# Two more chunks transposed by DMA instead of TensorE in a retention layer with a feed-forward block

## The chip, the cores and the metric

The kernel runs on one core of a Trainium2 chip. The metric is the time of one execution on the device in microseconds (us); where several executions were timed, their median is given. Engines are called as the profile calls them: PE is TensorE (PEld its weight loads), DVE is VectorE, ACT is ScalarE, POOL is GpSimd, and SP is the engine whose queue issues nearly all DMAs.

## The reference: what is computed

A recurrent retention layer (4 batches, 8 heads, 768 steps, head dimension 64) feeds a two-layer block with the activation h - tanh(h).

```python
gamma = 1.0 - 2.0 ** (-5.0 - np.arange(H))            # one decay for each head
for t in range(S):
    state = gamma * state + outer(k[:, :, t], v[:, :, t])
    y[:, :, t] = scale * (q[:, :, t] @ state)
x = y.transpose(0, 2, 1, 3).reshape(B * S, H * D)      # 3072 tokens of 512
h = x @ w_in                                           # 512 x 2048
out = (h - np.tanh(h)) @ w_out                         # 2048 x 512
```

q, k and v are float32. The two weight matrices arrive as 64-bit floats; the kernel converts them to float32 itself, in 32 tiles, with ACT, DVE and POOL.

## The kernel before

The 3072 tokens are 24 chunks of 128. For each chunk the kernel loads k, q and v, scales q and v by powers of the decay, and then needs k and q with the head dimension on the partitions (`kqT`), because the score products contract over it. There are two ways to get `kqT`.

With TensorE, as the kernel before does for chunks 0 to 7: eight transposes into a PSUM tile, and a copy out of it by ACT.

```python
    def turn(ci, which, early=False):          # which: 0 for k, 1 for q
        ...
            if which == 0:
                turned[ci] = banks("t", f"kqTp_{ci}")      # PSUM, tag "t" has one buffer
            tp = turned[ci][:, which]
        ...
        for p in range(NP):                    # NP = 4
            nc.tensor.transpose(tp[:, ts(p, P)],
                                t[:, ds(2 * p, 2)].rearrange("p h d -> p (h d)"), ident)

    def turn_copy(ci, which=None):
        ...
            nc.scalar.copy(out=t, in_=turned[ci].rearrange("p i (n t) -> p i n t", n=NP))
```

By DMA, as it does for chunks 8 to 23: ACT separates the 16-bit halves of the float32 words into `apart`, of which there is one buffer; one DMA stores them to a scratch in HBM; a second, transposing DMA reads the scratch and writes `kqT`.

```python
    def turn_by_dma(ci):
        apart = mid.tile([P, 2, 2, H * D], U16, tag="apart", name=f"apart_{ci}", bufs=1)
        for which in range(2):
            words = loaded[ci][which].rearrange("p h d -> p (h d)").bitcast(U16)
            nc.scalar.copy(out=apart[:, :, which],
                           in_=words.rearrange("p (n two) -> p two n", two=2))
        rows = dram.tile([P, 2, 2 * H * D], U16, tag="rows", name=f"rows_{ci}")
        nc.sync.dma_start(out=rows, in_=apart.rearrange("p two i n -> p two (i n)"))
        sides[ci] = mid.tile([P, 2, NP, P], F32, tag="kqT", name=f"kqT_{ci}")   # two buffers
        nc.sync.dma_start_transpose(
            out=sides[ci].rearrange("p i n t -> p (i n) t").bitcast(U16),
            in_=rows.rearrange("p two n -> (p two) n"),
        )
```

The chunk's further way: `products` (the k-v products, which do not read `kqT`, and then the scores, which do), `mask` and `state` on DVE, `outputs` and `outputs_rest` on TensorE, and `keep_x`, an ACT copy of the finished chunk into `xT`, from which the first layer's matmuls (`up`) read.

```python
    def products(ci):
        ...
                    nc.tensor.matmul(halves[...], kh[r, h], vh[r, h], ...)                       # L298
        ...
                    nc.tensor.matmul(halves[...], kT[r, p, ts(a, D)], qT[r, p, ts(a, D)], ...)   # L304

    def keep_x(ci):
        ...
        nc.scalar.copy(out=xT[n][:, :, ts(nj, P)]..., in_=y_banks[:, ci % 2]...)                 # L393

    def up(n, m2, i):
        ...
        keep_busy(hp[:, :P])
        for c in range(NC):
            nc.tensor.matmul(hp, w1[:, c, ts(2 * m2 + i, P)], xT[n // 2][:, c, ts(n % 2, TH)], ...)
```

`keep_busy` issues matmuls on a constant tile into a PSUM place that is about to be overwritten; their number is set by an `x` piece ahead of it. Chunks 4 to 7 are the tokens of `xT[1]`, and steps 4 and 5 of the feed-forward block read chunks 4 and 5.

Every engine runs its instructions in the order in which the program gives them. For the first eight chunks and the first steps of the feed-forward block that order is a string. A letter is a function, the number a chunk, weight tile or step: L loads a chunk, W a weight tile; s and w scale q and v; t and T transpose k and q on TensorE; c and C copy them out; p products, m mask, z state, b outputs, e a small read of the output by ACT, r the rest of the outputs, y keep_x; A, D, G convert a weight tile on ACT, DVE, POOL; u and v the two halves of `up`; a and q the activations of a step on ACT, d and g its DVE part; o the second layer's matmuls; E their sum; x idle matmuls.

```python
    order = """
    ...
    C4 r3 g0 L5 y3 x1 p4 A4 W5 u2 D3 s5 v2 W6 w5 m4 D4 u1 G3 a2 q2 z4 L6 x6 t5 d2 G4 T5 A5
    v1 W7 C5 g2 b4 s6 a1 W8 p5 w6 e4 u3 D5 q1 v3 m5 A6 G5 z5 r4 L7 a3 t6 d1 b5 W9 y4 T6 e5
    o0 s7 g1 C6 w7 A7 W10 D6 q3 r5 t7 W11 T7 D7 G6 y5 C7 x3 u4 d3 v4 G7 A8 g3 p6 a4 o1 A9 m6
    z6 q4 D8 p7 E1 d4 G8 b6 o2 e6 m7 g4 A10 r6 z7 u5 y6 D9 b7 v5 D10 G9 e7 r7 a5 o3 y7 q5
    G10 u6 E3 d5 A11 v6 g5 o4 a6 D11 q6 u7 G11 d6 v7 g6 o5 a7 q7 E5 d7 g7 W12 L8 W13 W14
    """
```

After this string a loop runs the other 88 steps and calls `turn_by_dma` for chunks 8 to 23.

Of the kernel before, what the change touches and what calls it, by code (L numbers as in the profile page):

```python
# [32 lines left out]
def kernel(  # L33
# [223 lines left out]
    def turn_copy(ci, which=None):  # L257
        if ci not in sides:
            sides[ci] = mid.tile([P, 2, NP, P], F32, tag="kqT", name=f"kqT_{ci}")
        t = sides[ci]  # L260
        if which is None:
            nc.scalar.copy(out=t, in_=turned[ci].rearrange("p i (n t) -> p i n t", n=NP))
        else:
            nc.scalar.copy(out=t[:, which],
                           in_=turned[ci][which].rearrange("p (n t) -> p n t", n=NP))
# [277 lines left out]
    def tall(ci):  # L543
# [8 lines left out]
        "T": lambda c: turn(c, 1, c < EARLY_TURNS),  # L552
        "c": lambda c: turn_copy(c, 0),
        "C": lambda c: turn_copy(c, 1 if c < EARLY_TURNS else None),
        "p": products,
        "m": mask,
        "z": state,
# [21 lines left out]
    m1 z1 y0 A1 D0 L2 x4 b1 t2 e1 c2 G0 r1 s2 y1 D1 x3 T2 w2 L3 u0 C2 W2 p2 G1 s3 t3 m2 T3  # L579
    w3 c3 v0 z2 C3 b2 A2 L4 p3 e2 W3 D2 a0 r2 s4 y2 w4 q0 W4 m3 z3 G2 x9 t4 b3 A3 d0 T4 e3  # L580
    C4 r3 g0 L5 y3 x1 p4 A4 W5 u2 D3 s5 v2 W6 w5 m4 D4 u1 G3 a2 q2 z4 L6 x6 t5 d2 G4 T5 A5
    v1 W7 C5 g2 b4 s6 a1 W8 p5 w6 e4 u3 D5 q1 v3 m5 A6 G5 z5 r4 L7 a3 t6 d1 b5 W9 y4 T6 e5
    o0 s7 g1 C6 w7 A7 W10 D6 q3 r5 t7 W11 T7 D7 G6 y5 C7 x3 u4 d3 v4 G7 A8 g3 p6 a4 o1 A9 m6
    z6 q4 D8 p7 E1 d4 G8 b6 o2 e6 m7 g4 A10 r6 z7 u5 y6 D9 b7 v5 D10 G9 e7 r7 a5 o3 y7 q5
    G10 u6 E3 d5 A11 v6 g5 o4 a6 D11 q6 u7 G11 d6 v7 g6 o5 a7 q7 E5 d7 g7 W12 L8 W13 W14
    """
# [101 lines left out]
```

## Time and profile before

| | before |
|---|---|
| time, median of 3 | 752.62 us (752.61 to 753.97) |
| span of the profiled execution | 752.1 us |
| PE busy | 740.9 us (99%) |
| DVE busy | 518.0 us (69%) |
| ACT busy | 389.4 us (52%) |
| POOL busy | 126.9 us (17%) |
| mean granted clock of TensorE | 0.998 |

The profile lists for each engine the busy time, and for groups of instructions the line of the kernel, the tile written and the tile read. A timeline gives start and length of merged instructions, and in brackets the idle time before them with what ended it. A table of stretches gives, for each, the busy time and number of instructions of an engine, the clock that TensorE was granted (1.00 is full), the busy share of the DMA engines and the rate. Engines that are idle without being the bottleneck cost nothing by that.

### The profile page before, as it was taken

Reading aid. Unit: us, or ns where it says so; the run is one execution under the profiler, and the core shown is the slowest. Engines: PE = TensorE matmul, PEld = TensorE weight load, DVE = VectorE, ACT = ScalarE, POOL = GpSimd, SP = SyncE. Lnnn points to the kernel's source line nnn. Section 1 sums busy time; section 2 is a strip of 40 time slices with the busy share of each in tenths; the row PEclk is TensorE's granted clock in tenths of the full one; section 3 lists DMA queues with packets and bytes.
Section 4 is the critical chain, followed back from the end, with each engine's and each line's share of the span. In section 5 each row is a group of like instructions: output and inputs, shape, how many; then the busy total and the mean of one; then the engine's idle time right before and its main releaser. Section 6 shows DMA issues by size and latency. Waiting matters only on the chain.

```text
span 752.1 us, 13885 instructions
## 1 busy us (share of the span) xinstructions
PE 740.9 (99%) x5502; PEld 509.9 (68%) x5502; DVE 518.0 (69%) x807; ACT 389.4 (52%) x727; POOL 126.9 (17%) x108
## 2 busy tenths in 40 slices
PE   8899999999999999999999999999999999999997
PEld 7786667666767676766676676666666666666775
DVE  4889989998898666656565656565665666656653
ACT  4567576667665546445545545444344434434442
POOL 0565445445444111100111100000000000000000
PEclk9999999999999999999999999999999999999999
DMA  9972436556553353343342421000000000000000
GB/s 196 234 182 74 127 89 172 158 158 153 156 128 84 99 155 107 67 96 93 91 99 71 98 58 56 29 1 1 29 0 1 28 1 0 29 0 1 28 2 28
DMA packets 125680, 59.76 MB, mean 79 GB/s; under 512 B 109872, under 2 KB 118576, under 8 KB 125616
## 3 DMA queue, kind: packets, MB, share of 16 engines
q1 hardware_dynamic: 125328, 58.67, 29.9%
q8 instruction: 43, 0.70, 0.4%
q10 hardware_dynamic: 288, 0.21, 0.1%
q14 instruction: 21, 0.17, 0.1%
HBM read 35.80 MB, written 14.68 MB: 67 GB/s over the span
## 4 chain that ended last, share of the span: by engine, by line
PE 96%; DMA 2%; DVE 1%; SPq 1%; ACT 0%; issue 0%; ACTq 0%; DVEq 0%
PE h L414 44%; PE o L462 42%; PE y L352 3%; PE o L470 2%; PE s L298 2%; PE s L304 1%; PE kqTp L212 1%; PE kqTp L250 1%; DMA raw<-in_moe_w_in_dram 1%; DMA k<-in_k_dram 1%; SPq L229 1%; DMA out_dram<-sum 0%; SPq L154 0%; DVE power L187 0%; DVE head L185 0%; DVE a L311 0%
## 5 line engine op out<-in xcount | busy, mean ns | idle before, releaser
L414 PE MATMUL h<-xT,w 128*128 128x256 f32 x1536 | 349.9, 381 | 0.0
L414 PEld LDWEIGHTS h<-xT,w 128*128 128x128 f32 x1536 | 289.7, 190 | 68.4 <-issue 31.8
L462 PE MATMUL o<-w,g 128*128 128x512 f32 x736 | 331.9, 593 | 0.0
L462 PEld LDWEIGHTS o<-w,g 128*128 128x128 f32 x736 | 139.4, 190 | 135.1 <-issue 128.4
L423 ACT ACTIVATE u<-h 128x512 f32<-128x512 f32 x96 | 57.3, 597 | 289.0 <-PE h L414 288.9
L439 DVE TENSOR_TENSOR th<-h,th 128x512 f32<-128x512 f32 x96 | 66.3, 690 | 176.0 <-ACT th L424 176.0
L453 DVE COPY_PREDICATED g<-large,th 128x512 f32<-128x512 int32 x96 | 71.8, 748 | 10.2 <-DVE g L452 0.5
L442 DVE SCALAR_TENSOR_TENSOR h<-q,h 128x512 f32<-128x512 f32 x96 | 66.8, 696 | 10.4 <-DVE h L440 0.5
L448 DVE SCALAR_TENSOR_TENSOR h<-q,h 128x512 f32<-128x512 f32 x96 | 66.6, 694 | 8.2
L431 ACT ACTIVATE q<-u,tab 128x512 f32<-128x512 f32 x96 | 69.4, 722 | 0.0
L432 ACT ACTIVATE q<-u,tab 128x512 f32<-128x512 f32 x96 | 69.1, 720 | 0.0
L433 ACT ACTIVATE large<-u,tab 128x512 f32<-128x512 f32 x96 | 68.8, 717 | 0.0
L452 DVE TENSOR_TENSOR g<-h,u 128x512 f32<-128x512 f32 x96 | 66.3, 691 | 3.3
L440 DVE SCALAR_TENSOR_TENSOR h<-u,h 128x512 f32<-128x512 f32 x96 | 65.8, 685 | 0.0
L236 POOL TENSOR_TENSOR q<-q,tab 128x512 f32<-128x512 f32 x22 | 24.3, 1104 | 198.4 <-DMA q<-in_q_dram 115.1
L424 ACT ACTIVATE th<-h 128x512 f32<-128x512 f32 x96 | 56.9, 592 | 0.0
L195 POOL TENSOR_TENSOR low<-low,power 128x512 f32<-128x512 f32 x30 | 38.5, 1282 | 103.1 <-DVE power L187 89.1
L199 POOL TENSOR_TENSOR w<-low,head 128x512 f32<-128x512 f32 x30 | 38.7, 1289 | 2.4
L352 PEld LDWEIGHTS y<-a,v 64*64 64x64 f32 x768 | 15.8, 134 | 16.7 <-ACT large L433 10.6
L236 POOL TENSOR_TENSOR v<-v,tab 128x512 f32<-128x512 f32 x22 | 26.5, 1207 | 0.1
L382 ACT COPY seen<-y 64x1 f32<-64x1 f32 x96 | 10.1, 153 | 28.2 <-PE y L352 27.8
L393 ACT COPY xT<-y 128x512 f32<-128x512 f32 x24 | 14.1, 587 | 17.0 <-PE y L352 17.0
(54 smaller groups left out, 412.8 us busy)
## 6 DMA issues: line engine op xcount, KB each, us to landing
rows<-apart SPq DMA_DIRECT2D x16, 512.0 KB, 2.8
k<-in_k_dram SPq DMA_DIRECT2D x24, 256.0 KB, 4.3
q<-in_q_dram SPq DMA_DIRECT2D x24, 256.0 KB, 4.9
v<-in_v_dram SPq DMA_DIRECT2D x24, 256.0 KB, 5.1
raw<-in_moe_w_out_dram SPq DMA_DIRECT2D x12, 512.0 KB, 3.6
out_dram<-sum SPq DMA_DIRECT2D x23, 256.0 KB, 2.1
raw<-in_moe_w_in_dram SPq DMA_DIRECT2D x14, 256.0 KB, 4.2
raw<-in_moe_w_in_dram SPq DMA_DIRECT2D x28, 128.0 KB, 3.9
```

The source lines that it names most:

```text
L414: nc.tensor.matmul(hp, w1[:, c, ts(2 * m2 + i, P)], xT[n // 2][:, c, ts(n % 2, TH)], start=(i == 0 and c == 0), stop=(c == NC - 1), skip_g ...
L423: nc.scalar.activation(u, hp, AF.Square)
L431: nc.scalar.activation(q0, u, AF.Square, bias=bias0)
L432: nc.scalar.activation(q1, u, AF.Square, bias=bias1, scale=math.sqrt(A))
L433: nc.scalar.activation(large, u, AF.Relu, bias=bias_m)
L439: nc.vector.tensor_tensor(th, hp, th, op=ALU.subtract)
L440: nc.vector.scalar_tensor_tensor(hp, in0=u, scalar=R, in1=hp, op0=ALU.subtract, op1=ALU.mult, reverse0=True)
L442: nc.vector.scalar_tensor_tensor(hp, in0=q0, scalar=C0, in1=hp, op0=ALU.add, op1=ALU.mult)
L448: nc.vector.scalar_tensor_tensor(hp, in0=q1, scalar=A * C1, in1=hp, op0=ALU.add, op1=ALU.mult)
L452: nc.vector.tensor_tensor(flat, hp, u, op=ALU.mult)
L453: nc.vector.copy_predicated(flat, large.bitcast(I32), th)
L462: nc.tensor.matmul(o_p[j], gT[n, m2][:, i, ts(j, P)], w2[:, 2 * m2 + i], start=(first and i == 0), stop=(last and i == 1))
```

## The change

Chunks 6 and 7 are transposed by DMA too: the pieces t6, T6, C6 and t7, T7, C7 go, and K6 and K7, which call `turn_by_dma`, come in. The load of chunk 7 and the loads of weight tiles 9, 10 and 11 are moved ahead of K6, so that on the SP queue they are issued before the store of chunk 6 to the scratch and the transposing DMA behind it. The aim is to take 16 transposes off TensorE, which is busy nearly all the time, and to spare ACT two copies out of PSUM.

```diff
         "C": lambda c: turn_copy(c, 1 if c < EARLY_TURNS else None),
+        "K": turn_by_dma,
         "p": products,
...
-    v1 W7 C5 g2 b4 s6 a1 W8 p5 w6 e4 u3 D5 q1 v3 m5 A6 G5 z5 r4 L7 a3 t6 d1 b5 W9 y4 T6 e5
-    o0 s7 g1 C6 w7 A7 W10 D6 q3 r5 t7 W11 T7 D7 G6 y5 C7 x3 u4 d3 v4 G7 A8 g3 p6 a4 o1 A9 m6
+    v1 W7 C5 g2 b4 s6 a1 W8 p5 w6 e4 u3 D5 q1 L7 W9 W10 W11 K6 v3 m5 A6 G5 z5 r4 a3 d1 b5 y4 e5
+    o0 s7 g1 w7 A7 D6 q3 K7 r5 D7 G6 y5 x3 u4 d3 v4 G7 A8 g3 p6 a4 o1 A9 m6
```

## The prediction

> **What bounds the kernel now.** I read the page first, then who waits for whom on TensorE (PE), then the chain of work in order of time around the places that the change touches, and last the timelines of ACT and of the SP queue there. The busy line of the page:
>
> ```profile
> PE 740.9 (99%) x5502; PEld 509.9 (68%) x5502; DVE 518.0 (69%) x807; ACT 389.4 (52%) x727; POOL 126.9 (17%) x108
> ```
>
> The span is 752.1 us, so PE stands still for only 11. The waits of PE say where: these are the longest two.
>
> ```profile
> PE kqTp L212 <- DVE state L327: 2.9, 1, 2.9
> PE y L352 <- issue: 1.5, 1, 1.5
> ```
>
> Both fall before 32 us. In the window from 40 us to the end, PE waits 0.5 us in all. So PE is the bound wherever the change works: what it takes off PE is gained in full, and what makes PE wait is lost in full, with no later slack to win it back. The chain in order of time (start, length, what) around the removed transposes:
>
> ```profile
> 54.66 0.39 PE y L352 x16
> 55.05 0.59 PE kqTp L250 x4
> 55.64 0.86 PE y L352 x48
> 56.50 0.59 PE kqTp L250 x4
> 57.09 3.44 PE o L462 x8
> 60.52 0.39 PE y L352 x16
> 60.91 1.02 PE kqTp L250 x8
> 61.94 0.67 PE h L212 x6
> 62.61 3.46 PE h L414 x16
> 66.06 0.62 PE s L298 x32
> ```
>
> L250 is the transposes of chunks 6 and 7, L212 the idle matmuls (x3), L414 step 4 (u4, v4), and L298 at 66.06 the products of chunk 6. ACT there:
>
> ```profile
> 52.55 0.66 ACT L172 ACTIVATE head<-raws 128x512 f32<-128x512 f32 x1
> 59.58 0.72 ACT L431 ACTIVATE q<-u,tab 128x512 f32<-128x512 f32 x1
> 60.80 0.72 ACT L433 ACTIVATE large<-u,tab 128x512 f32<-128x512 f32 x1
> 61.42 0.58 ACT L393 COPY xT<-y 128x512 f32<-128x512 f32 x1
> 61.97 1.01 ACT L262 COPY kqT<-kqTp 128x1024 f32<-128x1024 f32 x1
> ```
>
> L172 at 52.55 is the piece A6, which will have K6 ahead of it. L431 to L433 are q3, behind which K7 will stand. L393 is y5: it makes `xT` of chunk 5, and u4 reads that. Today y5 ends at 62.0, under the idle matmuls, and u4 waits for nothing. On the SP queue, the loads of weight tiles 9 to 11, and then the first store and transpose of the loop (chunk 8):
>
> ```profile
> 53.45 6.26 SPq L154 DMA_DIRECT2D raw<-in_moe_w_in_dram  x9
> ...
> 113.69 1.68 SPq L154 DMA_DIRECT2D raw<-in_moe_w_in_dram  x3
> 115.47 0.54 SPq L276 DMA_DIRECT2D rows<-apart  x1
> 119.41 1.87 SPq L278 DMA_TRANSPOSE kqT<-rows  x1
> ```
>
> The nine loads of W9 to W11 are already issued back to back behind chunk 7's load (from 50.6 us); they end at 59.71. The queue waits for no buffer among them: it is the issue itself that takes 6.26 us.
>
> [...] the transpose of chunk 8 is issued 3.9 us after its store, and the store's own median from issue to landing is 2.8 us (2.6 to 3.9; the 3.9 is the one right behind weight loads). [...] the input of y5 is there at 60.91, and y5 starts at 61.42, behind q3. [...] at the 2.9 us wait (columns: stretch, its length, PE busy and instructions, clock, DMA share, GB/s):
>
> ```profile
> 30.00:31.00 1.00, 0.00 (x0) 1.00 0.80 253
> 31.50:32.00 0.50, 0.50 (x5) 1.00 0.96 267
> 33.00:33.50 0.50, 0.50 (x4) 0.50 1.17 229
> 35.50:36.00 0.50, 0.50 (x20) 0.99 1.15 266
> ```
>
> PE resumes at 31.45, and from about 32.1 to 35.5, 3.4 us, it runs at half clock.
>
> **The change, part by part.**
>
> *Taken from PE:* the transposes of chunk 6, 0.59 + 0.59, and of chunk 7, 1.02: **2.20 us**, all on the path. PE would then be ready for u4 (idle matmuls included) at 62.61 - 2.20 = 60.4.
>
> *ACT:* two PSUM copies of 1.01 go; four copies into `apart` come. In the loop a pair takes 1.99 (the second starts 0.94 after the first and lasts 1.05). K6 stands behind q1, which ends at about 52.55; its inputs are there (q of chunk 6 was scaled by 47.4). So its copies run 52.55 to 54.54. A6, a3, y4, e5, A7 and q3 follow, at the spacings that they have now (1.15, 0.96, 0.48, 0.45, 1.15, 1.85): q3 ends at about 60.6. That chain alone is harmless so far.
>
> *SP:* the data of K6 are ready at 54.54, but its store stands behind W9 to W11, whose issue ends at 59.71. It is issued at 59.75. With the 3.9 us of the store that likewise stands behind weight loads, it lands at **63.7**. (The DMA engines are busy with W11 until 62.0, so the shorter 2.8 is not to be had; the 2.8 would give 62.6.)
>
> *The wait that comes in:* `apart` has one buffer. The copies of K7 write it, so they have to wait until the store of K6 has read it, at 63.7. And ACT is in order: y5, behind K7, waits with them. K7 63.7 to 65.75, y5 to 66.3, and u4, with 0.1 for the semaphores, starts at **66.4** in place of 62.61. PE, ready at 60.4, stands still for 6.0 us. Net of the 2.20 saved, u4 is **3.8 us later**.
>
> *The clock:* [...] 2.9 were enough above, so I expect half clock after it. At most a window of 3.4 us at half clock costs 1.7 us; part of it can fall into the stall[...]. I take **1.4**.
>
> *Do the transposes then come in time?* The transpose of K6 is issued at 63.7 and, at 4.2 us from issue to landing, lands at 67.9. The scores of chunk 6 start after u4 and v4, at 66.4 + 3.46 + 0.62 = 70.5 at the earliest: hidden. K7: store at 65.8, landing at about 69, transpose landed at about 73.2. Its scores come after o1 (3.63) and products, at 70.5 + 0.47 + 3.63 + 0.62 = 75.2: hidden, with 2 us to spare.
>
> *The early loads:* L7 and W9 to W11 start when they did, as the queue stands empty at 50 us and waits for the release of chunk 5's k. Their move gains no time by itself; it only puts the store of K6 last.
>
> Behind p7 all keep their order and spacing, and the loop does not change. Sum: 752.6 - 2.2 + 6.0 + 1.4 = **757.8 us**.
>
> **The rivals.**
>
> 1. *All hidden: only the 2.2 us count.* 750.4. For it: the loop does the same 16 times, and PE does not wait there once. Against it: in the loop the stores come 20 us apart, so `apart` has long been read; here the second use follows within 7 us, with three weight tiles ahead of the store.
> 2. *No wait for `apart`, only ACT's longer queue.* If the store landed before 60.6 (it would have to be issued before the weights), y5 would run 62.6 to 63.2, and u4 would start at 63.3: 6.0 - 3.1 = 2.9 us of stall against 2.2 saved, and perhaps no fall of the clock: 753 to 755.
> 3. *The transpose is late for the scores.* Under rival 2 or with a slow DMA the scores of chunk 6 would wait: they would stand ready at 63.3 + 3.46 + 0.62 = 67.4 against a landing at 67.9. Under my main case it costs nothing. For it to cost 2 us, the landing would have to take over 6 us; the 16 in the trace take 4.1 to 4.6.
> 4. *Something else comes free:* chunk 6 and 7 no longer pass through PSUM tag "t". No wait on it is seen after 40 us, so nothing is to be won.
>
> **Range and chances.** The stall of ACT follows from the program's order and one buffer; its length hangs on the store's landing (62.6 to 64.5: -1.1 to +0.8)[...]. Rival 2 gives the lower edge, both uncertain terms at their high end the upper: 754.4 to 760.0. About 1 in 10 I give to 750 to 754, rivals 1 and 2. A change of 2% would be 15 us, and no term is near that: faster 0.01, within 2% 0.97, slower 0.02.
>
> **What would show it.** Right: 16 transposes fewer on L250; an ACT idle stretch of about 3 us ahead of L273, at about 60.6, ended by DMA rows<-apart; a PE wait of some 6 us ahead of L414 at about 60.4, ended by ACT xT L393; a clock of 0.5 for some microseconds after it; no PE wait at L304 afterwards. Wrong: u4 without a wait (rival 1), a PE wait at L304 ended by DMA kqT (rival 3), a store of K6 issued ahead of 59 us, or full clock after the stall. If waits arise later, in the loop, the claim that nothing behind p7 changes has failed.

## The result and the profile after

| | before | after |
|---|---|---|
| median | 752.7 us (6 runs, 752.53 to 753.97) | 760.22 us (6 runs, 759.51 to 761.23) |
| ratio | 1 | 1.0097, interval 1.0084 to 1.0110 |
| span of the profiled execution | 752.1 us | 758.2 us |

The changed kernel is 7.5 us slower. The prediction was 757.8 us with a range up to 760.0, so the time lies 0.2 us above the range.

The busy line of the page: PE has 16 instructions fewer, as meant, and still more busy time, because its clock fell (mean 0.993 against 0.998).

```profile
PE 741.9 (98%) x5486; PEld 510.0 (67%) x5486; DVE 518.5 (68%) x807; ACT 391.3 (52%) x729; POOL 126.2 (17%) x108
```

The longest wait of PE and, in the window from 40 to 90 us, the wait of ACT behind it (who waited for whom: total, times, longest):

```profile
PE h L414 <- ACT xT L393: 6.6, 1, 6.6
```

```profile
ACT apart L273 <- DMA rows<-apart: 3.9, 1, 3.9
```

The SP queue in the changed kernel. The store of chunk 6 is issued behind the nine weight loads, and its transpose 4.6 us later:

```profile
52.53 6.24 SPq L154 DMA_DIRECT2D raw<-in_moe_w_in_dram  x9
58.87 0.54 SPq L276 DMA_DIRECT2D rows<-apart  x1
63.49 1.87 SPq L278 DMA_TRANSPOSE kqT<-rows  x1
```

ACT. The first line is the second copy of K6, ready 5.4 us before its store can be issued; then the two copies of K7, and y5 (L393) right behind them:

```profile
52.40 1.04 ACT L273 COPY apart<-q 128x1024 uint16<-128x1024 uint16 x1
...
63.55 1.05 ACT L273 COPY apart<-k 128x1024 uint16<-128x1024 uint16 x1 [3.92 <-DMA rows<-apart]
64.50 1.04 ACT L273 COPY apart<-q 128x1024 uint16<-128x1024 uint16 x1
65.57 0.58 ACT L393 COPY xT<-y 128x512 f32<-128x512 f32 x1
```

PE: u4 and v4 in one line, then the products of chunk 6 (L298):

```profile
66.20 6.15 PE L414 MATMUL h<-xT,w 128*128 128x256 f32 x16 [6.64 <-ACT xT L393]
72.28 0.69 PE L298 MATMUL s<-v,k 64*64 64x64 f32 x32
```

The scores (L304) follow at 72.80 with no wait: both transposes are in time. The same 16 rows (eight matmuls, each of which stands as two rows in the trace) took 3.46 us in the chain of before. The stretches (length, PE busy and instructions, clock, DMA share, GB/s) tell why:

```profile
64.00:65.00 1.00, 0.00 (x0) 0.66 0.04 9
...
67.00:68.00 1.00, 1.00 (x3) 0.50 1.10 411
...
71.00:72.00 1.00, 1.00 (x6) 0.92 1.00 216
```

PE has half its clock from about 64.3 to 71.1 us, 6.8 us, of which 4.9 lie after it has work again.

**The sum by parts.** The two profiled executions are not aligned: early on, where the two programs are the same, a wait of PE took 2.9 us in that of before and 1.5 in that of after, and each has a stretch at half clock of its own (32.1 to 35.5 before, 16.5 to 20.0 after). By chunk 5 the latter is 1.08 us ahead. I therefore measure from a mark that both have, the start of chunk 5's products on PE (49.90 and 48.82), up to the start of o2 (72.27 and 78.56). That stretch is 22.37 us before and 29.74 after, 7.37 more, close to the 7.5 of the medians. Within it, start to start:

| | before | after | difference |
|---|---|---|---|
| mark to the point where PE could start u4 | 12.54 | 10.48 | -2.06 |
| stall ahead of u4 | 0 | 6.90 | +6.90 |
| u4 and v4 | 3.55 | 6.08 | +2.53 |
| rest to o2 | 6.28 | 6.28 | 0.00 |

(The point after is 59.30: the idle matmuls start at 58.63 and take 0.67, as in the chain of before. The wait of 6.6 in the profile counts from their modelled end.)

### The profile page after: what moved, and what is told of

It reads as the page before. It is cut to its first block, busy times and chain, and to the rows that moved or that the text cites. A ratio compares the mean times of both kernels' runs of the same rounds, so it can differ in the third digit from the quotient of the medians.

```text
span 758.2 us, 13865 instructions
## 1 busy us (share of the span) xinstructions
PE 741.9 (98%) x5486; PEld 510.0 (67%) x5486; DVE 518.5 (68%) x807; ACT 391.3 (52%) x729; POOL 126.2 (17%) x108
## 4 chain that ended last, share of the span: by engine, by line
PE 95%; DVE 3%; ACT 1%; issue 0%; DMA 0%; POOL 0%; DVEq 0%; POOLq 0%
PE h L414 43%; PE o L462 41%; PE y L352 3%; PE o L470 2%; PE s L298 2%; PE s L304 1%; PE kqTp L212 1%; PE kqTp L250 1%; DVE head L185 1%; DVE head L183 1%; DVE power L187 0%; DVE head L181 0%; PE y L212 0%; DVE a L311 0%; DMA out_dram<-sum 0%
## 5 line engine op out<-in xcount | busy, mean ns | idle before, releaser
L393 ACT COPY xT<-y 128x512 f32<-128x512 f32 x24 | 14.1, 587 | 17.1 <-PE y L352 17.1
```

## The experiments

My theory has four links: the store behind the weight loads, the one buffer, the order on ACT, the clock. Five runs cut one link each (two of them the clock); two measure the gain alone; three put a better order together. Each ratio is to runs of before taken alongside, with medians of 752.39 to 752.70 us. "Stretch" is the length from chunk 5's products to o2 against 22.37 before. Line numbers move by up to 3 where lines were added.

| run | median, us | ratio to before (interval) | stretch against before |
|---|---|---|---|
| changed kernel | 760.22 | 1.0097 (1.0084 to 1.0110) | +7.37 |
| own buffer for chunk 7 | 755.9 | 1.0046 (1.0033 to 1.0058) | +3.21 |
| y5 ahead of K7 | 757.99 | 1.0068 (1.0056 to 1.0080) | +5.18 |
| 62 idle matmuls | 764.34 | 1.0153 (1.0140 to 1.0166) | +11.21 |
| 31 idle matmuls | 758.29 | 1.0078 (1.0065 to 1.0091) | +5.31 |
| no transposes of 6 and 7 | 751.94 | 0.9990 (0.9983 to 0.9996) | -0.55 |
| the same, less DVE work | 750.84 | 0.9978 (0.9970 to 0.9986) | -1.81 |
| store of 6 ahead of weights | 758.24 | 1.0076 (1.0062 to 1.0090) | +5.60 |
| three mends | 752.55 | 1.0001 (0.9993 to 1.0010) | -0.14 |
| weights 9, 10 early | 751.8 | 0.9987 (0.9979 to 0.9995) | -1.11 |
| and w7 late | 751.63 | 0.9984 (0.9977 to 0.9990) | not comparable, see below |

### The buffer: chunk 7's halves in a place of their own

```diff
-        apart = mid.tile([P, 2, 2, H * D], U16, tag="apart", name=f"apart_{ci}", bufs=1)
+        if ci == 7:      # a part of a weight staging tile that is free by then
+            apart = rooms[0][:, 0].bitcast(U16).rearrange("p (two i n) -> p two i n", two=2, i=2)
+        else:
+            apart = mid.tile([P, 2, 2, H * D], U16, tag="apart", name=f"apart_{ci}", bufs=1)
```

> The changed kernel, but chunk 7's 16-bit halves go to a buffer of their own (a part of a weight staging buffer that is free by then), so K7 need not wait for the store of chunk 6. My theory (the one buffer makes ACT wait 3.9 us, and y5 with it): the ACT wait ahead of K7 is gone, y5 ends 4 us earlier at about 62.2, PE waits 2.6 us ahead of u4 in place of 6.6, and the half clock is shorter or gone. What then shows is the next limit: the transposes land at 67.8 (chunk 6) and 73.8 (chunk 7) as before, so PE waits 1.5 and 1.3 us at the scores. In all 755 to 758 us. Rival (the ACT queue and the DMA latency themselves cost the time, the buffer does not): 760, no change.

755.9 us: 4.3 less than the changed kernel. The waits of PE in this run:

```profile
PE h L417 <- ACT xT L396: 2.6, 1, 2.6
PE s L307 <- DMA kqT<-rows: 1.8, 2, 1.1
```

The wait at u4 falls from 6.6 to 2.6 us, by the length of ACT's wait, and the clock stays at 1.00 in this profiled execution. It is the fastest of the six (755.27 us); the mean granted clocks of the other five are 0.992 to 0.997, so in those it fell somewhere. What is left is ACT's longer queue, and, only now in sight, transposes that land after their scores are ready. So the buffer is the cause of the long stall, but not the only thing that the place in the program costs.

### The order on ACT: y5 ahead of K7

```diff
-    o0 s7 g1 w7 A7 D6 q3 K7 r5 D7 G6 y5 x3 u4 ...
+    o0 s7 g1 w7 A7 D6 q3 r5 D7 G6 y5 K7 x3 u4 ...
```

> The changed kernel, with y5 and the conversion pieces ahead of K7 in the order; the one buffer stays. My theory: ACT still waits 3.9 us for the store of chunk 6, but y5 is through before, at about 60.2, and u4 starts at 60.3 (0.7 us of wait in place of 6.6). The scores of chunk 6 are then ready at 64.4 and wait for the landing at 67.8, 3.4 us, and those of chunk 7 for 73.8, 1.3 us. In all 752.7 - 2.0 + 0.7 + 3.4 + 1.3 = 756, up to 758 if the clock falls. Rival (it is not the order on ACT that held u4): u4 starts late as before, 760.

757.99 us. The waits of PE and, below, stretches with the clock as above:

```profile
PE s L304 <- DMA kqT<-rows: 3.1, 1, 3.1
...
PE h L414 <- ACT xT L393: 0.7, 1, 0.7
```

```profile
67.00:68.00 1.00, 0.37 (x12) 0.50 1.06 424
...
72.00:73.00 1.00, 1.00 (x2) 0.50 0.60 133
```

u4 waits 0.7 us, although ACT still waits (3.25 us) for the same store: the order was the link. The time goes to the next one, the scores of chunk 6, which wait 3.1 us for their transpose. And that wait, half as long as the one before, brings as long a fall of the clock: from 66.8 to 73.6 us, and o1, 3.63 us before, takes 6.1.

### The clock: idle matmuls in place of the wait

```diff
-    ... G6 y5 x3 u4 d3 ...
+    ... G6 y5 x62 u4 d3 ...      # first run; x31 in the second
```

> The changed kernel, with 62 idle matmuls ahead of u4 in place of 3, about 6.9 us at 0.112 each, which fill the wait for y5 and end just before it. The waits of the data stay as they are. My theory (the 16 matmuls of u4 and v4 take 6.15 us in place of 3.46 because the clock is halved after the wait): the clock stays at 1.00, u4 and v4 take 3.5 us, and the time falls by 2.7 us to 757.5. Rival (they are slow because the transposing DMA runs beside them, not through the clock): 6.15 us and 760 as before.

> As the run before with idle matmuls, with the number put right: 31, since each stands as two rows of 0.11 us in the trace, so that 62 took 13.9 us and outlasted the wait by 6.5. 31 take some 6.9 us and end just before y5. My theory (clock): u4 starts at 66.2 as in the changed kernel, u4 and v4 take 3.6 us in place of 6.15, and the time is 757.5. Rival (DMA beside it): 760.

The first number was wrong by a factor of two: an idle matmul stands as two rows, and 62 of them outlast the wait. They take 14.1 us, from 58.74. It tells half of what was asked, as u4 and v4 are fast again:

```profile
72.69 3.62 PE L414 MATMUL h<-xT,w 128*128 128x256 f32 x16
```

With 31, 58.21 to 65.4, the wait is filled and not outlasted. Timeline, and the stretch with the clock:

```profile
66.14 3.72 PE L414 MATMUL h<-xT,w 128*128 128x256 f32 x16 [0.75 <-ACT xT L393]
```

```profile
66.00:68.00 2.00, 1.86 (x9) 1.00 1.18 354
```

The clock is 1.00 beside the same transposing DMA (354 GB/s in this stretch), and from the start of u4 to the products of chunk 6 it takes 3.65 us in place of 6.08. So the clock made these matmuls slow, not the DMA. The median falls by 1.9 us (the stretch by 2.1) and not by the 2.7 expected: the clock gives 2.4 back, and in this profiled execution the store takes 5.2 us to land, so that u4 starts 0.4 us later after the mark.

### The gain alone: no transposes of chunks 6 and 7 at all

```diff
-        "K": turn_by_dma,
+        "K": lambda c: ...,     # chunks 6 and 7 take chunk 5's kqT: their transposes are left out
```

> Leaves out the transposes of chunks 6 and 7 altogether (neither TensorE nor DMA; these chunks use chunk 5's transposed k and q, so the output is not the reference's); the early loads stay. This measures the gain alone. My theory: 16 transposes are worth 2.0 to 2.2 us, nothing waits, 750.6 us. Rival (PE would only wait elsewhere for what the transposes covered): 752 or more.

751.94 us: 0.7 gained, not 2.0. PE in this run waits at a new place:

```profile
PE o L462 <- POOL w L199: 0.8, 1, 0.8
```

Its cause, on DVE and POOL of the same run (weight tile 7: the slowest of its steps on DVE, and the last on POOL):

```profile
60.30 1.64 DVE L185 SCALAR_TENSOR_TENSOR head<-raws,head 128x512 uint32<-128x512 uint32 x1
```

```profile
63.90 1.27 POOL L199 TENSOR_TENSOR w<-low,head 128x512 f32<-128x512 f32 x1
```

The second matmul of o1 needs that tile. In the profile of before POOL finished it at 66.69 (its last step 65.41 + 1.28), and that matmul came at about 67.9 (o1 at 67.08, and 0.86 for the first): a margin of 1.2 us, in which no wait is seen. Take away 2.06 us of PE, and the margin is used up, the more so as the tile is ready 0.4 us later after the mark (17.21 against 16.79); o1 takes 1.25 us longer from start to start than before. To see whether that is all, the next run leaves out half of tile 7's DVE work as well:

```diff
-        nc.vector.tensor_scalar(head.bitcast(F32), ..., HI_MIN, HI_MAX, ...)
-        nc.vector.tensor_scalar(head, head, 3, 0x3FFFFFF8, ...)
+        if i != 7:       # left out for tile 7: its weights are not the reference's
+            ...          # the same two operations
```

> As the run without transposes of chunks 6 and 7, and two of the four DVE operations on weight tile 7 (clamp and shift) are left out too, so these weights are not the reference's. In that run only 0.7 us of the 2.0 came through, and PE waited 0.8 us at o1 for weight tile 7's last step on POOL. My theory (DVE is the second bound here, and what PE saves is handed to a wait for it): the wait at o1 is gone and the time is 750.6 to 751.2. Rival (the transposes are worth only 0.7): 751.9 as in that run.

750.84 us, 1.1 less (0.9 by the ratios). o1 waits no longer:

```profile
67.33 3.70 PE L463 MATMUL o<-w,g 128*128 128x512 f32 x8
```

Most of the 2.06 us comes through: 1.81 in the stretch, 1.55 by the medians. So the transposes are worth nearly their 2 us on PE, and 0.7 of them was to be had with the rest as it is.

### The place on the SP queue: the store of chunk 6 ahead of the weights

```diff
-    ... D5 q1 L7 W9 W10 W11 K6 v3 ...
+    ... D5 q1 L7 K6 W9 W10 W11 v3 ...
```

> The changed kernel with weight tiles 9 to 11 behind K6 instead of ahead of it; chunk 7's load stays ahead; the one buffer stays. My theory: the store of chunk 6 is issued at 53.4 as soon as its copies are done and lands at about 56.5, ahead of K7, so ACT does not wait for the buffer; y5 ends at 62.2, PE waits 2.7 us at u4 for ACT's longer queue, and none at the scores of chunk 6; chunk 7's store now stands behind the weights, and its scores wait about 1.5 us. 755, and up to 757 if the clock falls. Rival (the place on the SP queue does not matter, the buffer is read late anyhow): 760.

```profile
52.99 0.36 SPq L276 DMA_DIRECT2D rows<-apart  x1
...
64.22 0.54 SPq L276 DMA_DIRECT2D rows<-apart  x1
70.45 1.35 SPq L278 DMA_TRANSPOSE kqT<-rows  x1
```

And of the waits of PE in this run:

```profile
PE s L304 <- DMA kqT<-rows: 2.4, 1, 2.4
```

The store of chunk 6 lands at 56.4, K7 does not wait for the buffer, and the wait at u4 is 2.6, as expected and as with the second buffer. But now chunk 7's store stands behind the same nine loads and takes 6.2 us to land, longer than I had reckoned with; its scores wait 2.4 us. In the profiled execution (758.93 us) the clock falls at both waits (to 0.5 from 61.5 to 64.9 and from 75.1 to 78.5). So 758.24 and not 755, above the 757 that I gave for a fall of the clock: of the two stores, the one behind the weight loads paid (4.6 us to land for chunk 6's in the changed kernel, 6.2 here for chunk 7's).

### A better order

Three mends in one: own buffer; only tile 9 ahead of K6; K7 and y5 ahead of q3.

```diff
-    ... D5 q1 L7 W9 W10 W11 K6 v3 ...
-    o0 s7 g1 w7 A7 D6 q3 K7 r5 D7 G6 y5 x3 u4 ...
+    ... D5 q1 L7 W9 K6 v3 ...
+    o0 s7 g1 w7 A7 D6 K7 W10 W11 r5 y5 q3 D7 G6 x3 u4 ...
```

> All three mends in one: chunk 7's halves have a buffer of their own; only weight tile 9 stays ahead of K6, tiles 10 and 11 go behind K7; and K7 and y5 stand ahead of q3 on ACT. My theory: y5 ends at 60.3, PE waits 0.7 us at u4 and nowhere else after it, 752.6 - 2.0 + 0.7 = 751.3 to 752. Rival (the path by DMA is too slow for this place in the program, whatever the order): waits at the scores of chunk 6 or 7, 754 or more.

752.55 us, the time of before, 0.5 to 1.2 above what I expected. PE waits three times for small amounts: 0.8 us at u4, about 0.2 at the scores of chunk 6, and, listed here, 0.3 at those of chunk 7:

```profile
PE s L307 <- DMA kqT<-rows: 0.3, 1, 0.3
```

Then tiles 9 and 10 ahead of chunk 7's load, where the queue stands empty, tile 11 behind K7, and y5 ahead of K7:

```diff
-    ... s6 a1 W8 p5 ... q1 L7 W9 W10 W11 K6 v3 ...
-    o0 s7 g1 w7 A7 D6 q3 K7 r5 D7 G6 y5 x3 u4 ... v4 G7 A8 ...
+    ... s6 a1 W8 W9 W10 p5 ... q1 L7 K6 v3 ...
+    o0 s7 g1 w7 A7 D6 r5 y5 K7 W11 q3 D7 G6 x3 u4 ... v4 G7 A8 ...
```

> As the combined run, but weight tiles 9 and 10 are loaded ahead of chunk 7, where the SP queue stands empty from 44 to 49 us; tile 11 goes behind K7; and y5 stands ahead of K7 as well as of q3. My theory: chunk 6's store is issued at 53.0 and chunk 7's at 60.6 with nothing ahead of them; both transposes land ahead of their scores (about 60.7 and 67.5), y5 is in time, and the only wait left is that at o1 for weight tile 7 (POOL, 0.8 us, as in the run that leaves the transposes out): 751.4 to 752.0, a little faster than before. Rival (the loads ahead delay chunk 7 and K7 with it): a wait at chunk 7's scores, 752.5 or more.

751.8 us, faster than before by 0.05% to 0.21%. Neither u4 nor a score waits. o1 is longer by 0.4 (4.08 in place of 3.70):

```profile
65.10 4.08 PE L465 MATMUL o<-w,g 128*128 128x512 f32 x8
```

Last, with the scaling of v of chunk 7 behind tile 7 on POOL:

```diff
-    o0 s7 g1 w7 A7 ... v4 G7 A8 ...
+    o0 s7 g1 A7 ... v4 G7 w7 A8 ...
```

> As the run with early weight loads, and POOL's scaling of v of chunk 7 is moved behind the last step of weight tile 7. Beside that scaling the first DVE operations of weight tile 6 took 1.25 and 1.15 us in place of 0.42 and 0.43. My theory (DVE's conversion of tiles 6 and 7 is the second bound): it is ready some 0.7 us earlier, the wait at o1 goes to about 0.1, and the time is 750.7 to 751.4. Rival: the wait only moves, 751.4 to 752.0.

751.63 us, not to be told from the 751.8 of the run before, and short of what I expected. The profiled execution, at 753.79 us the slowest of the 21, cannot tell whether the move helped. o1 takes its 3.7 us again, but PE comes to it late, because of a wait within u3 that no other profile has:

```profile
PE h L417 <- issue: 2.0, 1, 2.0
```

The clock fell behind it (0.50 from 52.3 to 55.7), and o1 starts 19.1 us after the mark, against 15.5 in the run before; weight tile 7 is ready at 17.0, against 16.7. The profile shows nothing that PE waited for in u3. How often that wait comes in the other executions, and why, stays open.

## Why the prediction was right and where it failed

- **Bound and place: right.** PE's path sets the end, and what happened between 50 and 73 us explains the whole difference, 7.37 of 7.5 us. Nothing changed after p7: from the start of o2 to the end it is 679.8 us before and 679.6 after.
- **The chain of causes: right, link by link.** The store behind the weight loads, ACT held by the one buffer, y5 behind K7, PE held by y5; both scores in time. The three runs that cut a link each (own buffer, y5 first, store first) left 2.6, 0.7 and 2.6 us of the stall at u4.
- **Saving: 2.20 said, 2.06 measured.** But "what it takes off PE is gained in full" was wrong. The stall hid this in the changed kernel; without the stall only 0.7 us came through, and in that trace o1, waiting for weight tile 7, is 1.25 us longer. I took the absence of waits for free room; a margin of 1.2 us looks the same.
- **Stall: 6.0 said, 6.9 measured.** The term that was too small is the landing of the store: 3.9 us taken from the one store in the loop that stands behind three loads, 4.6 behind nine. (In the other runs that issue it behind the same nine loads it took 4.2 to 5.2; behind chunk 7's loads alone 3.4 with the store ahead of the weights, and 4.3 with weights 9 and 10 early. So the number of loads ahead is not all that sets it.) The store's issue was a further 0.2 later after the mark; the rest, K7, y5 and the start of u4, 2.65 against 2.7, was right.
- **Clock: 1.4 said, 2.5 measured.** The step that failed is "At most a window of 3.4 us at half clock costs 1.7 us". I had one stretch at half clock from the profile of before (32.1 to 35.5) and took its length as the most that one stall costs, an estimate. Here the half clock lasted twice as long: 6.8 us, of which 4.9 lay after the stall.
- **The sum.** The mechanism was right, and two terms were too small: the clock by 1.1 us and the stall by 0.9. With only one of them too small the time would have been 759.1 or 759.3 us, inside the range; it took both. With 2.5 and 6.9 in place of 1.4 and 6.0 the sum is 752.7 - 2.1 + 6.9 + 2.5 = 760.0. Of the range above 757.8, 0.8 us is for the landing; the rest, up to 760.0, was my estimate for the clock, and no trace of before showed it. The lower edge, 754.4, follows from no sum that is shown.
- **Rivals.** Rival 1 (750.4) sized the gain as if nothing else were near: 751.94. Rival 2 (no wait for the buffer, 753 to 755, said with the store ahead of the weights) was built in two ways, with an own buffer and with that store first. In both the stall at u4 is 2.6 us, close to the 2.9 said, but waits at the scores of 1.8 and 2.4 us come on top: 755.9 and 758.24. Rival 3 had those waits by itself. Its own sum sets scores that are ready at 67.4, because the store landed before 60.6, against the landing at 67.9 of a store that lands at 63.7; with the early store the transpose would land at about 64.8 (60.6 and 4.2), and in the run with the store first the scores of chunk 6 indeed do not wait. Of rival 4, "No wait on it is seen after 40 us, so nothing is to be won": no run tests it for PSUM, and for o1 the same reasoning failed, as above.

## What to carry to other kernels

When a busy engine is relieved, look for the work whose result it takes up just in time, not only for its waits: here a weight tile that came 1.2 us ahead of its use let only 0.7 of 2 us through. A copy into a single buffer ties the engine that makes it to the transfer that reads that buffer: here ACT waited 3.9 us for a store, and y5, behind the copy, with it. So put ahead of such a copy whatever the engine owes to the critical path (with y5 ahead the wait at u4 fell from 6.6 to 0.7 us). Issue bulk loads where no store that something waits for stands behind them on the same queue, as here in the empty stretch ahead of chunk 7's load (no wait at u4 or a score was left). Where a stall of several microseconds on TensorE is foreseen, count the clock too: behind waits of 6.6 and 3.1 us it was halved for 6.8 us here. Or fill the stall with idle matmuls that end just before the data come: 31 of them kept the clock at 1.00 in the profiled execution here and took 1.9 us off the median.

## What the runs showed of the hardware

The length of a wait did not set the length of the half clock in these traces. A wait of 6.6 us went with 6.8 us of half clock (64.3 to 71.1, the first 1.9 still within the wait), one of 3.1 us with as much (66.8 to 73.6, y5 first), waits of 2.9 (before), 2.6 and 2.4 (store ahead of weights) and 2.0 us (w7 late) with 3.4 each, and one of 2.6 us (own buffer, 58.8 to 61.4) with none.

Nor did PE's return end it at once. From the moment that PE had work again, the half clock went on for 4.9 us in the changed kernel (from 66.2), for 6.0 with y5 first (from 67.6), and for 3.2 with the store ahead of the weights (from 61.7 to 64.9).

What decides between none, 3.4 and 6.8 us was not shown: no run searched for it.
